# One load instead of four for the last V tile, and 256 rows of w4 in loads of 62, 2 and 64 partitions

## The chip, the cores and the metric

The kernel runs on one core of a Trainium2 chip. The metric is the device time of one execution in microseconds (us). Before the change the median of three runs is 196.03 us (195.90 to 196.08).

## The reference

One token is decoded for a batch of 8, with a width of 512. The first half is attention over a window: 32 query heads share 8 key/value heads, and of a cache of 8192 positions only the last 2048 count. The second half is a gated residual block whose token-shift branch is zero for a sequence of one token, so that w1 and w2 are never needed. What is left:

```
h  = x + attention(layernorm(x)) @ wo          # K and V: 8 x 8 x 2048 x 128 bf16 each
z  = layernorm(h)
x1 = z                                         # the shifted parts are zero for S = 1
h2 = h + x1 + gelu(layernorm(x1) @ w3) @ w4    # w3: 512 x 1792, w4: 1792 x 512
```

All arrays are bf16. The K and V windows are 67 MB of the 79 MB that the kernel reads.

## The kernel before

**Tiles.** K and V come in 16 units each (`NUN` = 16: 8 batches by 2 halves of the key/value heads). A unit is a load of 2 MB: 128 partitions, 16 KB in each, one contiguous run per partition. `knat` and `vnat` hold four such units each. Every unit of K is turned on the PE (line 305), moved out of PSUM by ACT and DVE (lines 292 and 293), and multiplied with the queries (line 320). After the softmax of a batch, V is multiplied with the probabilities (`pe_PV`, line 411 for the last three units, line 421 for the others).

**Order of the work.** There is no planner. Each engine has a list of operations written out by hand, and `Engine.emit` puts a wait in front of an operation where its list of (semaphore, value) pairs asks for one. All large loads are issued from SP's queue in one order: wq, then K and V units in turn (V three units behind K), the first half of wo at units 5 and 9, and at the end V of units 13, 14 and 15, the second half of wo in four pieces, w3 in four pieces, w4 in four pieces. An SP load waits until the buffer that it writes is free; the w3 and w4 loads go into the K buffers 0 and 1, which are free long before.

**The last V unit.** `load_v` loads units 0 to 14 in one DMA with runs of 16 KB. Unit 15 is loaded in four DMAs (lines 478 to 480), each a quarter of the columns, with runs of 4 KB per partition and a semaphore each (`sem_vl`). `V(n, w)` (line 396) gives `pe_PV` the semaphore for quarter w, so the PE can start on a quarter when it has landed.

**w4.** w4 has 1792 rows, that is 14 blocks of 128. Rows 0 to 1535 come in three DMAs of 512 rows: partition p gets four consecutive rows, a run of 4 KB. The first two have one semaphore (`sem_w4a`, wait for 32), the third `sem_w4b`. The last 256 rows come in a fourth DMA, two rows, 2 KB, per partition (lines 610 and 611, `sem_w4c`). In what follows these are called w4a (two pieces), w4b and w4c.

**The end of the chain.** After V the PE adds wo (line 498), DVE and ACT make the two layer norms (lines 619 to 649), the PE multiplies with w3 (line 639), DVE and ACT make the gelu in two halves (lines 655 and 657), and the PE multiplies with w4 (line 667) in groups that wait in this order: 32 blocks of 128x128 for `sem_w4a` and the gelu, 16 for `sem_w4b`, 8 for `sem_w4c`. Then come an addition, a turn, a copy and the store of 8 KB.

Of the kernel before, what the change touches and what calls it, by code (L numbers as in the profile page):

```python
# [21 lines left out]
F = 1792  # L22
FC = F // 128
# [7 lines left out]
U = 4  # L31
RR = 32
NCU = W // RR
UL = NCU * DH

NK = 4
NV = 4
# [44 lines left out]
def bass_sequential_preLN__sliding_block_cached__mixer_s_mlp__decode_kernel(  # L82
# [19 lines left out]
    NUN = NB * NU  # L102
# [4 lines left out]
    with es:  # L107
        sb = lambda shape, dtype, name: es.enter_context(nc.sbuf_tensor(name, shape, dtype))
        ps_t = lambda shape, dtype, name: es.enter_context(nc.psum_tensor(name, shape, dtype))
        S = lambda name: es.enter_context(nc.semaphore(name))  # L110

        knat = sb([128, NK, UL], dt.bfloat16, "knat")
        vnat = sb([128, NV, UL], dt.bfloat16, "vnat")
# [4 lines left out]
        w4_sb = knat[:, 1, 0:FC * D].rearrange("p (c n) -> p c n", c=FC)  # L118
# [49 lines left out]
        def tl(n, bf=False):  # L168
# [19 lines left out]

        sem_k = [S(f"sem_k{i}") for i in range(NK)]
        sem_v = [S(f"sem_v{i}") for i in range(NV)]  # L190
        sem_vl = [S(f"sem_vl{i}") for i in range(U)]
        sem_wl = [S(f"sem_wl{i}") for i in range(2)]
        sem_x, sem_wq, sem_wo, sem_w3, sem_w4a, sem_w4b, sem_w4c, sem_out = (
            S(n) for n in ("sem_x", "sem_wq", "sem_wo", "sem_w3", "sem_w4a", "sem_w4b", "sem_w4c", "sem_out"))
        PE, AC, DV, PO, SP = (Engine(S(n)) for n in ("s_pe", "s_act", "s_dve", "s_pool", "s_sp"))

        def dma(eng, dst, src, sem, *waits):
            def f(e):
                e.dma_start(dst, src).then_inc(sem, 16)  # L199
            eng.op(f, *waits, inc=False)  # L200
# [81 lines left out]
        e_T, e_Tlo, e_Thi, e_lo, e_hi, e_QK, e_PV = {}, [], [], [], [], {}, {}  # L282
# [111 lines left out]
            e_rL[b] = DV.op(lambda e: e.tensor_tensor(rLk[:, s, :, :], r_bc, k_bc, ALU.mult), e_r, e_mK)  # L394

        def V(n, w):
            if n == NUN - 1:
                return sem_vl[w], 16
            return sem_v[n % NV], 16 * (n // NV + 1)

        e_ev_o, e_fold = {}, {}
# [1 line left out]
        def pe_PV(i):  # L403
            n, w = divmod(i, U)
            b, t = divmod(n, NU)

            def f_last(e):
                for c in range(16):
                    cc = 8 * (w % 2) + c // 2
                    o = 256 * (cc // 2) + 32 * (4 * t + 2 * (w // 2) + c % 2) + cc % 2  # L410
                    ins = e.matmul(oT_ps[:, 0:16], vnat[:, n % NV, (16 * w + c) * DH:(16 * w + c + 1) * DH],  # L411
                                   pS[:, b % 2, o:o + 31:2], start=(w == 0 and c == 0), stop=(w == U - 1 and c == 15),
                                   skip_group_check=True)
                return ins

            def f(e):
                for c in range(8):
                    cc = 8 * (w % 2) + c
                    o = 256 * (cc // 2) + 32 * (4 * t + 2 * (w // 2)) + cc % 2
                    q = c % TO  # L420
                    ins = e.matmul(oT_ps[MO * q:MO * (q + 1), NO * (n % 2):NO * (n % 2 + 1)], pS[:, b % 2, o:o + 2 * MO - 1:2],  # L421
                                   vnat[:, n % NV, (16 * w + 2 * c) * DH:(16 * w + 2 * c + 2) * DH],
                                   start=(w == 0 and c < TO), stop=(w == U - 1 and c >= 8 - TO),
                                   tile_position=(0, MO * q), skip_group_check=True)
                return ins
            e_PV[i] = PE.op(f if n < NUN - NST else f_last, V(n, w), *e_pS[b],
                            e_ev_o.get(n - 1), e_sc[n - 1] if n > NUN - NST else None)
# [44 lines left out]
        def load_v(n):  # L472
            b, t = divmod(n, NU)
            src = A_v_cache[b, J * t:J * (t + 1), W0:SK, :].rearrange("j (r c) d -> r j (c d)", r=RR)
            if n < NUN - 1:
                dma(SP, vnat[:, n % NV, :], src, sem_v[n % NV], e_PV.get(U * (n - NV + 1) - 1))
                return
            for w in range(U):
                cs = slice(w * UL // U, (w + 1) * UL // U)
                dma(SP, vnat[:, n % NV, cs], src[:, :, cs], sem_vl[w], e_PV.get(U * (n - NV + 1) - 1))  # L480

        def load_wo(m, sem, g=2):
            dma(SP, wo_v[:, m:m + g, :, :].rearrange("p g k n -> p g (k n)"),
# [51 lines left out]
        for n in range(NUN):  # L535
# [4 lines left out]
            if n >= LVD:  # L540
                load_v(n - LVD)
            if n in WO_AT:
                load_wo(WO_G[WO_AT.index(n)], sem_wo)
            i = U * n
# [35 lines left out]
        for n in range(NUN - LVD, NUN):  # L580
            load_v(n)
# [22 lines left out]
            dma(SP, w3_sb[:, k, :], B_w3[128 * k:128 * (k + 1), :], sem_w3, e_T[U * (NUN - NK + 1) - 1])  # L604
        FA = 12
        w4_a = B_w4[0:FA * 128, :].rearrange("(a p c) n -> p a (c n)", p=128, c=4)
        for a, sem in ((0, sem_w4a), (1, sem_w4a), (2, sem_w4b)):
            dma(SP, w4_sb[:, 4 * a:4 * a + 4, :].rearrange("p c n -> p (c n)"), w4_a[:, a, :], sem,
                e_T[U * (NUN - NK + 2) - 1])
        dma(SP, w4_sb[:, FA:FC, :].rearrange("p c n -> p (c n)"),  # L610
            B_w4[FA * 128:F, :].rearrange("(p c) n -> p (c n)", c=FC - FA), sem_w4c)

        v3 = lambda t: t.rearrange("p (n b) -> p n b", b=B)
        vr = lambda t: t.rearrange("p (n b) -> p b n", b=B)
# [38 lines left out]
        for n in range(2):  # L653
            cs = slice(n * FH * B, (n + 1) * FH * B)
# [5 lines left out]
        for lo, hi, waits in ((0, FH, (e_gT[0], e_exp[NB - 1], (sem_w4a, 32))),  # L660
                              (FH, 8, (e_gT[1],)),
                              (8, FA, ((sem_w4b, 16),)),
                              (FA, FC, ((sem_w4c, 16),))):
            def pe_w4(e, lo=lo, hi=hi):
                for fc in range(lo, hi):
                    for nb in range(KC):
                        ins = e.matmul(z_ps[:, nb * B:(nb + 1) * B], w4_sb[:, fc, nb * 128:(nb + 1) * 128],
                                       gT[:, fc * B:(fc + 1) * B], start=(fc == 0 and nb == 0),
                                       stop=(fc == FC - 1), skip_group_check=True)
                return ins  # L670
            e_z = PE.op(pe_w4, *waits)
# [44 lines left out]
```

## Time and profile before

| | |
|---|---|
| median of three runs | 196.03 us |
| the profiled execution's own time | 195.93 us |
| its span in the trace | 194.6 us |
| DMA: bytes, mean over the span | 79.46 MB, 408 GB/s |
| share of the span in which PE / DVE / ACT are busy | 75% / 51% / 46% |
| last landing of w3 | 187.44 us |
| last landing of w4a, w4b, w4c | 189.95, 191.22, 191.85 us |
| last PE block of w4 ends | 192.29 us |

Times of single events count from the start of the span. The trace holds, for every DMA, when it was issued and when each of its 16 increments of the semaphore landed; a load is there when the last of the 16 has landed. It also holds every packet that the DMA engines moved, with start, duration and bytes, but not the number of the engine. The packets of one engine follow each other closely: the next one starts 3 to 4 ns before the one before has ended. As every engine has its own offset, the 16 chains can be told apart, and are called chain 0 to 15 here, in the order in which they began with wq.

### The profile page before, as it was taken

The numbers are of one execution on the slowest core, as the hardware profiler recorded it, in microseconds if no ns is written. First come the engines' busy times: TensorE is split into PE (matmuls) and PEld (weight loads), VectorE is DVE, ScalarE is ACT, GpSimd is POOL, SyncE is SP. The second block draws the span as 40 slices with busy tenths as digits, with TensorE's granted clock in tenths as the row PEclk, the third lists the DMA queues.
The fourth block names the chain that finished last, engine by engine and source line by source line (L and its number), as shares of the span: only waits on it lengthen the run. The fifth ranks groups of instructions, "written<-read, shape, count | busy, mean of one in ns | idle before, by whom it ended". The sixth has DMA issues, their size and how long they took to land.

```text
span 194.6 us, 4466 instructions
## 1 busy us (share of the span) xinstructions
PE 145.5 (75%) x1971; PEld 114.9 (59%) x1971; DVE 99.8 (51%) x256; ACT 89.2 (46%) x113; POOL 7.4 (4%) x28
## 2 busy tenths in 40 slices
PE   0038985988999794969497988785597896878764
PEld 0037852665777564756495857473585674767753
DVE  5402444784767492649055385565255865631130
ACT  6000565863847453655244646472264564150040
POOL 5001001001000100010001000100000000000000
PEclk9999999999999999999669699999799999555555
DMA  6999999999999999999999999999999999999981
GB/s 217 431 431 431 428 431 431 424 431 426 424 404 448 428 426 424 431 418 424 428 414 428 424 428 424 431 421 426 428 428 428 431 424 428 415 401 406 407 352 51
DMA packets 7538, 79.46 MB, mean 408 GB/s; under 512 B 856, under 2 KB 864, under 8 KB 3424
## 3 DMA queue, kind: packets, MB, share of 16 engines
q1 hardware_dynamic: 7504, 79.18, 96.9%
q8 instruction: 15, 0.25, 0.5%
q14 instruction: 3, 0.02, 0.0%
q10 hardware_dynamic: 16, 0.01, 0.0%
HBM read 79.18 MB, written 0.01 MB: 407 GB/s over the span
## 4 chain that ended last, share of the span: by engine, by line
DMA 51%; PE 30%; DVE 9%; SPq 6%; ACT 2%; issue 2%
DMA knat<-in_A_k_cache_dram 43%; PE kT_ps L305 18%; DMA knat<-in_B_w_dram 8%; SPq L199 6%; PE S_ps L320 5%; DVE kT_sb L293 5%; PE kT_ps L377 3%; DVE mcol L330 1%; DVE Pz L366 1%; PE sm L439 1%; ACT kT_sb L292 1%; ACT P_sb L351 1%; DVE Mrow L336 1%; PE sm L334 1%; PE sm L385 1%
## 5 line engine op out<-in xcount | busy, mean ns | idle before, releaser
L292 ACT ACTIVATE kT_sb<-kT_ps 128x1024 bf16<-128x1024 bf16 x64 | 62.8, 1023 | 43.4 <-PE kT_ps L305 43.4
L305 PE MATMUL kT_ps<-perm_k,knat 128*128 128x128 f32 x512 | 71.6, 298 | 11.3 <-DMA knat<-in_A_k_cache_dram 10.8
L305 PEld LDWEIGHTS kT_ps<-perm_k,knat 128*128 128x128 f32 x512 | 63.6, 154 | 19.0 <-DMA knat<-in_A_k_cache_dram 13.0
L293 DVE TENSOR_SCALAR kT_sb<-kT_ps 128x512 int32<-128x512 int32 x64 | 43.7, 689 | 37.7 <-PE kT_ps L305 37.7
L320 PE MATMUL S_ps<-kT_sb,qz 128*32 128x512 bf16 x256 | 19.9, 384 | 6.7 <-DVE kT_sb L293 3.9
L366 DVE TENSOR_TENSOR Pz<-P_sb,mJ 128x256 bf16<-128x256 bf16 x64 | 23.9, 416 | 0.0
L421 PE MATMUL oT_ps<-vnat,pS 128*32 128x256 bf16 x416 | 17.7, 280 | 0.9 <-DMA vnat<-in_A_v_cache_dram 0.9
L430 ACT ACTIVATE oE<-oT_ps 128x256 f32<-128x256 f32 x13 | 5.0, 384 | 27.4 <-PE oT_ps L421 27.4
L292 ACT ACTIVATE pS<-kT_ps 128x1024 bf16<-128x1024 bf16 x8 | 8.2, 1024 | 10.3 <-PE kT_ps L377 10.3
L421 PEld LDWEIGHTS oT_ps<-vnat,pS 128*32 128x32 bf16 x416 | 9.3, 97 | 4.1 <-DMA vnat<-in_A_v_cache_dram 1.0
L320 PEld LDWEIGHTS S_ps<-kT_sb,qz 128*32 128x32 bf16 x256 | 4.6, 94 | 11.6 <-ACT kT_sb L292 10.9
L293 DVE TENSOR_SCALAR pS<-kT_ps 128x512 int32<-128x512 int32 x8 | 5.5, 692 | 10.2 <-PE kT_ps L377 10.2
L377 PE MATMUL kT_ps<-perm_p,Pz 128*128 128x128 f32 x64 | 9.6, 298 | 0.0
L377 PEld LDWEIGHTS kT_ps<-perm_p,Pz 128*128 128x128 f32 x64 | 7.6, 151 | 3.0 <-issue 3.0
L259 PE MATMUL S_ps<-xlnT,wbig 128*128 128x8 bf16 x128 | 3.6, 168 | 7.7 <-DMA wbig<-in_A_wq_dram 7.7
L277 POOL COPY qz<-q_sb 64x64 bf16<-64x64 bf16 x16 | 4.6, 290 | 117.5 <-PE S_ps L320 101.7
L330 DVE TENSOR_REDUCE mcol<-S_ps 128x1 f32<-128x512 f32 x8 | 5.5, 692 | 5.8 <-PE S_ps L320 5.8
L259 PEld LDWEIGHTS S_ps<-xlnT,wbig 128*128 128x128 bf16 x128 | 3.5, 104 | 7.7 <-issue 7.7
L439 PEld LDWEIGHTS sm<-selo,oE 128*128 128x128 f32 x52 | 7.6, 211 | 0.4 <-ACT oE L430 0.4
L439 PE MATMUL sm<-selo,oE 128*128 128x16 f32 x52 | 7.6, 260 | 0.3 <-DVE negcol L348 0.3
L411 PE MATMUL oT_ps<-pS,vnat 128*128 128x16 bf16 x192 | 6.2, 174 | 1.7 <-DVE oK L445 1.0
L411 PEld LDWEIGHTS oT_ps<-pS,vnat 128*128 128x128 bf16 x192 | 5.9, 105 | 2.4 <-DMA vnat<-in_A_v_cache_dram 1.2
(90 smaller groups left out, 84.7 us busy)
## 6 DMA issues: line engine op xcount, KB each, us to landing
knat<-in_A_k_cache_dram SPq DMA_DIRECT2D x16, 2048.0 KB, 30.2
vnat<-in_A_v_cache_dram SPq DMA_DIRECT2D x15, 2048.0 KB, 34.3
wbig<-in_A_wq_dram SPq DMA_DIRECT2D x1, 4096.0 KB, 12.2
wbig<-in_A_wo_dram SPq DMA_DIRECT2D x2, 1024.0 KB, 33.0
vnat<-in_A_v_cache_dram SPq DMA_DIRECT2D x4, 512.0 KB, 10.8
wbig<-in_A_wo_dram SPq DMA_DIRECT2D x4, 512.0 KB, 12.6
knat<-in_B_w_dram SPq DMA_DIRECT2D x4, 448.0 KB, 13.6
knat<-in_B_w_dram SPq DMA_DIRECT2D x3, 512.0 KB, 15.1
```

Source lines behind the costliest of these rows:

```text
L199: e.dma_start(dst, src).then_inc(sem, 16)
L259: ins = e.matmul(S_ps[0][:, h * B:(h + 1) * B], wq_v[:, kc, h * DH:(h + 1) * DH], xlnT[:, kc * B:(kc + 1) * B], start=(kc == 0), stop=(kc ...
L292: e_lo.append(AC.op(lambda e: e.activation(dst[:, 0:1024], ps[:, 0:1024], ACT.Copy), e_Tlo[k], *free))
L293: e_hi.append(DV.op(lambda e: e.tensor_single_scalar(dst[:, 1024:2048].bitcast(dt.int32), ps[:, 1024:2048].bitcast(dt.int32), 0, ALU.bitwi ...
L305: ins = e.matmul(ps[:, c * 128:(c + 1) * 128], src[:, c * 128:(c + 1) * 128], perm_k[:, :], is_transpose=True)
L320: ins = e.matmul(S_ps[b % 2][32 * j:32 * (j + 1), :].rearrange("p (c r) -> p c r", c=16), qz[:, b % 2, J * t + j, k, lo:lo + 32], kT[:, j, k],
L330: e_max[b] = DV.op(lambda e: e.tensor_reduce(mcol[:, :], S_ps[b % 2][:, :], AX.X, ALU.max), e_QK[4 * b + 3], e_mT.get(b - 1))
L366: e_Pz[b, part] = DV.op(lambda e, o=o, p_bc=p_bc, m_bc=m_bc: e.tensor_tensor(Pz[:, 0, J * o:J * (o + 64)].rearrange("p (x j k) -> p x j k" ...
L377: ins = e.matmul(ps[:, c * 128:(c + 1) * 128], src[:, c * 128:(c + 1) * 128], perm_p[:, :], is_transpose=True)
L411: ins = e.matmul(oT_ps[:, 0:16], vnat[:, n % NV, (16 * w + c) * DH:(16 * w + c + 1) * DH], pS[:, b % 2, o:o + 31:2], start=(w == 0 and c = ...
L421: ins = e.matmul(oT_ps[MO * q:MO * (q + 1), NO * (n % 2):NO * (n % 2 + 1)], pS[:, b % 2, o:o + 2 * MO - 1:2], vnat[:, n % NV, (16 * w + 2 ...
L439: ins = e.matmul(sm[:, 32:48], oE[:, o:o + 128], selo[:, 16 * s:16 * s + 16], start=(s == 0), stop=(s == 2 * VP - 1))
```

## The change

V of unit 15 is loaded as the other units are, in one DMA with runs of 16 KB, with the semaphore of its buffer; `sem_vl` is gone, and all of unit 15's products wait for the whole unit. w4c is cut into three DMAs by partitions: 0 to 61, 62 and 63, and 64 to 127. The first two are issued after w3 and ahead of w4a; the third is issued last, where w4c was. All three count on `sem_w4c`, and the last eight PE blocks wait for 48 instead of 16.

```diff
-        sem_vl = [S(f"sem_vl{i}") for i in range(U)]
...
         def V(n, w):
-            if n == NUN - 1:
-                return sem_vl[w], 16
             return sem_v[n % NV], 16 * (n // NV + 1)
...
         def load_v(n):
...
-            if n < NUN - 1:
-                dma(SP, vnat[:, n % NV, :], src, sem_v[n % NV], e_PV.get(U * (n - NV + 1) - 1))
-                return
-            for w in range(U):
-                cs = slice(w * UL // U, (w + 1) * UL // U)
-                dma(SP, vnat[:, n % NV, cs], src[:, :, cs], sem_vl[w], e_PV.get(U * (n - NV + 1) - 1))
+            dma(SP, vnat[:, n % NV, :], src, sem_v[n % NV], e_PV.get(U * (n - NV + 1) - 1))
...
         w4_a = B_w4[0:FA * 128, :].rearrange("(a p c) n -> p a (c n)", p=128, c=4)
+        w4_c = B_w4[FA * 128:F, :].rearrange("(p c) n -> p (c n)", c=FC - FA)
+        for a, z in ((0, 62), (62, 64)):
+            dma(SP, w4_sb[a:z, FA:FC, :].rearrange("p c n -> p (c n)"), w4_c[a:z, :], sem_w4c,
+                e_T[U * (NUN - NK + 2) - 1])
         for a, sem in ((0, sem_w4a), (1, sem_w4a), (2, sem_w4b)):
             dma(SP, w4_sb[:, 4 * a:4 * a + 4, :].rearrange("p c n -> p (c n)"), w4_a[:, a, :], sem,
                 e_T[U * (NUN - NK + 2) - 1])
-        dma(SP, w4_sb[:, FA:FC, :].rearrange("p c n -> p (c n)"),
-            B_w4[FA * 128:F, :].rearrange("(p c) n -> p (c n)", c=FC - FA), sem_w4c)
+        dma(SP, w4_sb[64:128, FA:FC, :].rearrange("p c n -> p (c n)"), w4_c[64:128, :], sem_w4c)
...
-                              (FA, FC, ((sem_w4c, 16),))):
+                              (FA, FC, ((sem_w4c, 48),))):
```

## The prediction

> **What bounds the kernel now.** I read the slices of the page first.
>
> ```profile
> DMA  6999999999999999999999999999999999999981
> GB/s 217 431 431 431 428 431 431 424 431 426 424 404 448 428 426 424 431 418 424 428 414 428 424 428 424 431 421 426 428 428 428 431 424 428 415 401 406 407 352 51
> DMA packets 7538, 79.46 MB, mean 408 GB/s; under 512 B 856, under 2 KB 864, under 8 KB 3424
> ```
>
> The DMA engines are busy in every slice until the last two, so the time is set by bytes, by what a packet costs, and by what follows the last landing. The chain that ended last says which landing:
>
> ```profile
> 176.01 15.22 DMA knat<-in_B_w_dram
> 191.22 0.05 issue
> 191.27 0.59 PE S_ps L667 x16
> 191.86 0.04 issue
> 191.90 0.39 PE S_ps L667 x8
> ```
>
> It is w4b, at 191.22. The sixteen blocks that wait for it end at 191.86; w4c landed at 191.85, so the last eight follow with no more gap than an issue. The DMA view of 187 to 192 us, in 40 slices, shows how the end is reached:
>
> ```profile
> DMA  9899999896765666647469344443334332100000
> ...
> q8 instruction: 1, 0.02, 1.3%
> ```
>
> From 188 on the share falls in steps: engines run dry one after the other. The 16 increments for w4c land at 188.39 to 188.73 (six of them), 189.46, 190.10, 190.38, 190.84, and 191.50 to 191.85 (six). The packet records say why. In the run there are 15 instruction fetches of 16 KB (q8) and 3 of 8 KB (q14); a fetch of 16 KB takes 1.0 to 1.1 us, holds up the engine's own packets and leaves it about 1.1 us behind for good. Followed along the chains, q8 goes round eight engines in a fixed order (chains 5, 10, 6, 14, 3, 13, 11, 8), q14 hits two more (9, 9 and 1), and six are never hit (0, 2, 4, 7, 12, 15). Those six finish 3.3 us early. The stage behind w4 is this, in the timeline:
>
> ```profile
> 187.22 1.28 ACT L657 ACT_TABLE_LOAD   x1
> ...
> 187.49 1.97 PE L639 MATMUL kT_ps<-Pz,knat 128*128 128x8 bf16 x56 [0.75 <-DMA knat<-in_B_w_dram]
> ...
> 188.87 0.25 ACT L657 ACTIVATE Pz<-Pz 128x56 bf16<-128x56 f32 x1 [0.36 <-DVE Pz L655]
> ...
> 190.09 0.99 PE L667 MATMUL S_ps<-Pz,knat 128*128 128x8 bf16 x32 [0.62 <-ACT Pz L657]
> ...
> 191.27 1.01 PE L667 MATMUL S_ps<-Pz,knat 128*128 128x8 bf16 x24 [0.18 <-DMA knat<-in_B_w_dram]
> ```
>
> The wait before 190.09 is put down to ACT, but the gelu had ended at 189.12; w4a landed at 189.95.
>
> **The change, part by part.** The sum is made against the profiled execution: 195.93 us, of which 1.3 lie outside the span of 194.6. The median, 196.03, is 0.10 higher.
>
> *V of unit 15 in one load.* In the packet records a 4 KB packet follows the last after 158.2 ns, a 16 KB one after 610, a semaphore's after 6. Each engine spent 32 x 158.2 + 4 x 6 = 5.09 us on this unit and will spend 8 x 610 + 6 = 4.89: everything behind it lands 0.20 us earlier. (The first landings of units 13, 14 and 15 bear it out: 164.35, 169.25, 174.34.) SP issues three DMAs fewer (0.60 us each), in a queue that is ahead of the data by 10 to 15 us: nothing.
>
> The four quarters landed by 174.03, 175.31, 176.59 and 177.87; the PE began on the first at 176.79 and was through at 178.88. Now it begins when the whole unit is there, 177.87 - 0.20 + 0.05 = 177.72, and needs the same 2.09: 179.81, or 0.93 later. Behind it on the PE stand wo (line 498), the layer norm's sums and w3. What covers this: the first w3 block waited 0.75 us for w3's landing at 187.44 while its input was ready at 185.53, so 0.93 later is still in time for 187.24. On ACT the gelu's table load moves from 187.22 to 188.15, the first gelu ends at 189.68 instead of 189.12, and w4a lands at 189.75: hidden, with 0.1 us to spare. If more is lost on the way, it is paid one for one (rival 3).
>
> *w4c by partitions.* A packet of 2 KB follows the last after 80.5 ns. The piece of 64 to 127 gives each of 16 engines 4 packets instead of 8, so a late engine ends 0.32 us earlier: w4c at 191.85 - 0.20 - 0.32 = 191.33. But w4b lands at 191.02, and its 16 blocks run to 191.66: w4c is no longer waited for, and is worth 0.04 us at most.
>
> *The 62 rows.* How many engines take them? The trace has one short load: x, 8 rows, had 8 data packets and 8 semaphore packets on 8 engines, one row each. In every load the engines have equal shares (each chain holds 466 packets). Equal shares of 62 rows are possible on 2 engines with 31 each or on one; the 2 rows then go to two as well. Bounds: spread over 16 engines, 4 rows are 0.32 us; on two, 32 rows. I take two, since no load here has unequal shares. [...]
>
> On those two, w4a and w4b now stand behind 32 x 80.5 + 12 = 2.59 us more. This is the lower bound. The upper one comes from whether another engine can write a partition at full speed while the engine that always serves it is writing. In all loads with 128 partitions each engine has its own eight, so the trace never shows two engines on the same ones. An engine runs at 16384 B / 610 ns = 26.9 GB/s; if that is also what its partitions can take, two share it and a row costs 161 ns, 32 rows 5.15 us. The nearest row is x: five 1 KB rows for neighbouring partitions set out their semaphore packets within 41 ns (one packet alone is 44 ns) but land over 90 ns, 2.08 to 2.17; the 16 increments of the output store are 13 ns apart. They seem to queue. I take the upper bound less the four rows for an engine's own partitions: 28 x 161 + 4 x 80.5 + 12 = 4.84 us. [...]
>
> The sum, if the two are never-hit engines: their w4a ended at 186.04 to 186.34 (second piece, before its 0.42 us to landing), so it lands at 186.04 - 0.20 + 4.84 + 0.42 = 191.10 to 191.40. The 32 blocks run from 191.15 to 192.14. w4b, 1.27 later, lands at 192.37 to 192.67; its blocks run from 192.42 to 193.01. The last piece, 4 rows more, lands 0.33 to 0.65 later at 192.7 to 193.3, the eight blocks end at 193.44 to 193.7 instead of 192.29: **+1.15 to +1.45, I take +1.3**: 197.2, 197.3 against the median.
>
> SP issues two DMAs more (0.43 to 1.09 us each by the rows at 168 to 179 us) but is 10 us ahead; without that lead they would cost up to 2.2 us. The longer wait (48) stands last on the PE, nothing is queued behind it but the tail, which is unchanged.
>
> **The rivals.**
>
> 1. *The two engines are never-hit ones and write at full speed.* Then w4b is at 187.74 - 0.20 + 2.59 = 190.1 on them, ahead of the late engines' 191.02, and the end is 191.02 + 0.05 + 0.59 + 0.39 = 192.05: -0.24 us, 195.8 (-0.12%). For it: 3.3 us of idle time fit 2.59. It decides as long as a row costs under 115 ns (3.68 us from 187.54 to 191.22, by 32). Spreading 62 rows over many engines gives the same 195.8.
> 2. *One of the two is an engine that fetches.* Six chains of 16 end 3 us later than the idle ones. At 80.5 ns a row, w4b lands at 191.02 + 2.59 = 193.61, the end is 194.68: +2.4, 198.4; with sharing up to 200.7. Chain 1 or 9 (q14) lies between: 196.0 to 198.9. [...] I give it 0.22.
> 3. *Unit 15's later start is not hidden.* There is an idle stretch of 1.05 us in wo at 179.56 with nothing waited for, after a fetch (178.12 to 179.20). If the delay of 0.93 brings on another such gap, the gelu is 1.0 late beyond its cover and the w4 blocks run without waits from 190.8 to 192.8: +0.5, 196.5.
>
> **How the numbers follow.** A change of 0.2% (0.39 us) is about what can be told from none. Forecast (two prompt engines, shared writing) 0.40; rival 1 with the spread rows 0.33; rival 2 0.22; rival 3 0.05. Rival 1 gains less than 0.2%, so most of it is "same", some 0.07 of it faster if more than 0.39 is gained. Slower: 0.40 + 0.22 + 0.04 = 0.66. The likeliest one's own range is 196.6 (sharing costs 70%) to 197.8. To hold 8 in 10 the range goes from 195.7 (rival 1) to 198.8 (rival 2 without sharing); the rest of rival 2 is left out above, a larger gain below.
>
> **What would show it.** In the changed profile: the packets under 8 KB fall from 3424 by some 550 (unit 15's 512 data packets and 48 of semaphores go); first landing of unit 15 at 174.14; the 62-row load has 62 packets with two late increments; where the two chains spend 160 ns per 2 KB packet, the forecast holds, at 80 rival 1. PE's L667 groups then wait for w4a and w4b at 191 and 192. If the last engines of w4b are chains with two fetches and 32 rows, it was rival 2. Wrong altogether: w4b landing earlier than 191.02 on all engines, or a PE that waits for wo, not for w4.

## The result and the profile after

The changed kernel takes 197.14 us (median of six runs, 197.05 to 197.59) against 196.03 before: a ratio of 1.0061, 95% interval 1.0051 to 1.0072. The profiled execution took 197.29 us, its span is 196.0, 1.4 more than before.

The page of the changed kernel (DMA rows, all 40 slices):

```profile
DMA  6999999999999999999999999999999999999980
GB/s 236 428 421 428 435 428 428 428 428 426 421 415 428 428 428 423 428 425 428 420 426 428 428 428 428 428 421 426 425 425 428 431 425 428 425 413 395 378 265 35
DMA packets 7110, 79.46 MB, mean 405 GB/s; under 512 B 812, under 2 KB 820, under 8 KB 2868
```

Up to the 37th slice it is nearly the same kernel. In the 38th and 39th (4.9 us each) the engines are as busy as before, and move 378 and 265 GB/s where they had moved 407 and 352. The packets under 8 KB are 556 fewer: the single load of V has 560 fewer, and the new loads of w4 have 4 more of semaphores.

The chain that ended last, in order of time:

```profile
178.18 14.64 DMA knat<-in_B_w_dram
192.82 0.05 issue
192.86 0.82 PE S_ps L662 x24
```

It still ends in w4b, which landed at 192.82 instead of 191.22. w4c's last piece landed at 192.97, in time for the last eight blocks, so the PE's last 24 blocks follow without a gap. The timeline of the tail (start, duration, operation, idle time before it and what ended that):

```profile
177.85 0.60 PE L408 MATMUL oT_ps<-pS,vnat 128*128 128x16 bf16 x16 [1.27 <-DMA vnat<-in_A_v_cache_dram]
...
178.51 1.45 PE L408 MATMUL oT_ps<-pS,vnat 128*128 128x16 bf16 x48
...
188.28 1.99 PE L634 MATMUL kT_ps<-Pz,knat 128*128 128x8 bf16 x56 [1.38 <-DMA knat<-in_B_w_dram]
...
191.32 1.00 PE L662 MATMUL S_ps<-Pz,knat 128*128 128x8 bf16 x32 [1.05 <-DMA knat<-in_B_w_dram]
...
192.86 0.81 PE L662 MATMUL S_ps<-Pz,knat 128*128 128x8 bf16 x24 [0.55 <-DMA knat<-in_B_w_dram]
```

The PE now starts V of unit 15 at 177.85, as the sum had it (177.72). Then it waits for data three times: for w3 until 188.28 (before: 187.49), for w4a until 191.32 (190.09), for w4b until 192.86 (191.27). That w3 is late is the sign to follow up: the w3 loads stand ahead of the new loads in the queue. It does not set the end itself: both halves of the gelu had ended by 190.81, and w4a landed at 191.18.

The start of wo, before:

```profile
179.00 0.56 PE L498 MATMUL S_ps<-o,wbig 128*128 128x8 bf16 x15
180.62 1.47 PE L498 MATMUL S_ps<-o,wbig 128*128 128x8 bf16 x49 [1.05 <-issue]
```

and after:

```profile
180.09 2.15 PE L490 MATMUL S_ps<-o,wbig 128*128 128x8 bf16 x64
```

One stretch, 185 to 188.5 us, with the busy time (and number of instructions) of PE, its weight loads, DVE, ACT and POOL, the granted clock, and two columns on DMA; before the change:

```profile
185.00:188.50 3.50, 1.91 (x34) 1.73 (x34) 1.43 (x8) 1.70 (x3) 0.00 (x0) 0.50 0.97 384
```

and after it:

```profile
185.00:188.50 3.50, 1.27 (x10) 1.09 (x11) 1.43 (x8) 1.54 (x3) 0.00 (x0) 0.50 1.02 290
```

The last two columns are the share of time in which the DMA engines are busy and the GB/s. All 16 are busy and move a quarter less. In the packet records the chains of two engines each show 31 packets of 2 KB, a semaphore's, one more of 2 KB: one chain from 183.56 to 186.90, the other from 184.24 to 187.76. From 185.5 until about 189 most packets take 1.2 to 1.7 times their usual time (0.16 us for 4 KB before the change), and they do so on all 16 chains alike (up to 188, 1.4 to 1.6 times in the mean of each chain).

### The profile page after: what moved, and what is told of

It reads as the page before. It is cut to its first block, busy times and chain, and to the rows that moved or that the text cites. A ratio compares the mean times of both kernels' runs of the same rounds, so it can differ in the third digit from the quotient of the medians.

```text
span 196.0 us, 4465 instructions
## 1 busy us (share of the span) xinstructions
PE 146.9 (75%) x1971; PEld 116.4 (59%) x1971; DVE 99.5 (51%) x256; ACT 89.6 (46%) x113; POOL 7.4 (4%) x28
## 4 chain that ended last, share of the span: by engine, by line
DMA 52%; PE 28%; DVE 9%; SPq 7%; ACT 2%; issue 2%
DMA knat<-in_A_k_cache_dram 44%; PE kT_ps L304 16%; DMA knat<-in_B_w_dram 7%; SPq L198 7%; PE S_ps L319 5%; DVE kT_sb L292 5%; PE kT_ps L376 3%; DVE mcol L329 1%; DVE Pz L365 1%; ACT kT_sb L291 1%; PE sm L436 1%; ACT P_sb L350 1%; DVE Mrow L335 1%; PE sm L333 1%; PE sm L384 1%
## 5 line engine op out<-in xcount | busy, mean ns | idle before, releaser
L304 PE MATMUL kT_ps<-perm_k,knat 128*128 128x128 f32 x512 | 72.9, 302 | 10.8 <-DMA knat<-in_A_k_cache_dram 10.4
L304 PEld LDWEIGHTS kT_ps<-perm_k,knat 128*128 128x128 f32 x512 | 65.1, 157 | 18.2 <-DMA knat<-in_A_k_cache_dram 12.5
```

The costliest lines, as they stand in the source:

```text
L304: ins = e.matmul(ps[:, c * 128:(c + 1) * 128], src[:, c * 128:(c + 1) * 128], perm_k[:, :], is_transpose=True)
```

## The experiments

Theory 1: rows for partitions that another engine serves are what slows. Theory 2: two engines with long queues of short rows slow the rest, whichever the partitions. Besides, V's later start could be the cost.

**The two parts alone.** The V part alone is the change without its w4 edits; the w4 part alone is the change with `sem_vl` and the four V loads put back.

> V of unit 15 in one load, w4 as before. By my theory (the loss is all in the w4 loads) everything behind unit 15 lands 0.20 us earlier, the PE starts unit 15 at 177.8 instead of 176.8 and is covered, and the time falls by 0.2 us to about 195.8. By the rival that the later start of unit 15 costs the time: 0.5 to 1.0 us slower than before, w3 or the gelu waiting for the layer norm.

> w4's last rows as in the changed kernel (62, 2, 64), V of unit 15 in four loads as before. By my theory the whole loss is here: 197.2 to 197.4, 0.2 above the changed kernel at most, and the data moved per us falls to some 260 to 350 GB/s for 3 to 4 us from the moment the two loads begin. By the rival that V costs the time: 195.9 to 196.1.

V alone: 195.80 us (median of 11) against 196.06, ratio 0.9993 (0.9984 to 1.0002). w4 alone: 197.47 us, ratio 1.0074 (1.0059 to 1.0090). The loss is in the w4 loads: +1.41 there and -0.26 for V make +1.15, and the change measured +1.11. The -0.26 is a difference of medians; the interval of V alone includes 1, so that a gain is not shown, but a loss of 0.5 us or more is excluded. In the profile of V alone, unit 15 starts on the PE at 177.85 and the PE later waits 1.14 us for w3 (before: 0.75); its last landings are 187.72 for w3 and 191.48 for w4b in that execution, which was the second longest of its runs (196.14).

**Where the rows go.** All further kernels but the last are V alone with something added ahead of w4a. The first adds two loads of 2 partitions by 16 rows of 2 KB into spare buffers (the store at the end waits for them too; they have landed by then in every run):

```diff
+        for h in range(2):
+            dma(SP, knat[h:h + 5:4, 2:4, :].rearrange("p k (i n) -> p (k i) n", n=1024),
+                A_wo.rearrange("(g i t r) n -> g i t (r n)", i=16, t=2, r=2)[2 * h:2 * h + 2, :, 0, :], sem_d, e_T[NBLK - 1])
```

The second adds the same rows in the shape of the change, to 62 and 2 partitions:

```diff
+        for a, z in ((0, 62), (62, 64)):
+            dma(SP, knat[a:z, 2, 0:1024], A_wo.rearrange("(x t r) n -> x t (r n)", t=2, r=2)[a:z, 0, :], sem_d, e_T[NBLK - 1])
```

> V of unit 15 in one load and w4c in one load of 128 partitions (so e1), and ahead of w4a two extra loads of 2 partitions by 16 rows of 2 KB, into spare buffers, whose results nobody uses: again 32 rows on each of two engines, but into partitions 0, 1 and 4, 5, which by the even split of a 128-partition load may be the two engines' own. Theory 1 (foreign partitions are what slows): rows go at 80 ns each, no other engine slows, the two end about 2.6 us later, still before or with the late ones; 195.8 to 196.3. Theory 2 (two engines with long queues of 2 KB rows slow the rest, whatever the partitions): the same fall to 260 to 350 GB/s as in the changed kernel, 197.0 to 197.8.

> As the run with rows into partitions 0, 1, 4, 5, with the same source rows, but the extra loads go to partitions 0 to 61 and 62 to 63, one row of 2 KB each. Theory 1 and theory 2 both expect the fall in GB/s and 197.0 to 197.8; a third, that the w4 rows themselves or their place in memory are the cause, expects 195.8 to 196.3 here.

Into partitions 0, 1, 4, 5: 195.80 us, ratio 0.9989 (0.9980 to 0.9998), no loss at all. Into 0 to 63: 196.92 us, ratio 1.0046 (1.0032 to 1.0060). The 128 KB are the same, the source is the same, and so, by their place in time, are the two engines (each time one chain of 32 rows begins at 183.3 to 183.4, and a second about 0.75 later). With partitions 0, 1, 4, 5, 16 rows take 1.32 to 1.33 us on either, 83 ns each. The stretch of 185 to 188.5 again, with partitions 0, 1, 4, 5:

```profile
185.00:188.50 3.50, 2.23 (x38) 2.04 (x39) 1.44 (x9) 1.52 (x3) 0.00 (x0) 0.50 0.97 383
```

and with 0 to 63:

```profile
185.00:188.50 3.50, 1.11 (x15) 0.92 (x16) 1.43 (x8) 1.71 (x3) 0.00 (x0) 0.50 1.03 303
```

Theory 2 falls, and the loss comes without w4's own rows, their place in memory or their semaphore. What is left between the two is the partitions: either that most belong to other engines, or that every row has a new one.

**Foreign or many.** The same two loads again, into partitions 8, 9, 12 and 13, and later into 32, 33, 36 and 37:

```diff
-            dma(SP, knat[h:h + 5:4, 2:4, :].rearrange("p k (i n) -> p (k i) n", n=1024),
+            dma(SP, knat[8 + h:13 + h:4, 2:4, :].rearrange("p k (i n) -> p (k i) n", n=1024),
```

> As the run with rows into partitions 0, 1, 4, 5 (which measured 195.80 and no fall in GB/s), but into partitions 8, 9, 12, 13: still two engines, two partitions at a time and 16 rows of 2 KB in each, only that the partitions are ones that two other engines should serve. Theory 1 (foreign partitions): a fall in GB/s, rows of 100 to 160 ns, and 196.4 to 197.2. A theory that it is the many partitions (a new one with every row) expects no fall and 195.7 to 196.1.

> As the runs with rows into partitions 0, 1, 4, 5 (no fall) and 8, 9, 12, 13 (fall to 205 GB/s), now into 32, 33, 36, 37. If an engine's own partitions are eight in a row (0 to 7, 8 to 15), these are foreign: a fall to about 205 GB/s and some 198.2. [...]

Partitions 8, 9, 12, 13: 198.21 us, ratio 1.0103 (1.0086 to 1.0120), the slowest of all and 1 us beyond the range that theory 1 was given. Partitions 32, 33, 36, 37: 195.80 us, ratio 0.9985 (0.9974 to 0.9996). In the stretch of 185 to 188.5, with 8, 9, 12, 13:

```profile
185.00:188.50 3.50, 1.19 (x4) 1.00 (x4) 1.69 (x10) 1.19 (x3) 0.00 (x0) 0.50 1.01 200
```

and with 32, 33, 36, 37:

```profile
185.00:188.50 3.50, 1.88 (x35) 1.69 (x35) 1.42 (x8) 1.71 (x3) 0.00 (x0) 0.50 0.96 380
```

So it is not the number of partitions, which is four each time: it is which four (198.21 us with 8, 9, 12, 13, and 195.80 with each of the other two sets). Nothing else about 8, 9, 12 and 13 is slow, as every load of 128 partitions writes them too, and there no chain falls behind other than by a fetch. The reading that fits these runs is that the two engines' own partitions include 0, 1, 4, 5 and 32, 33, 36, 37, and not 8, 9, 12, 13, so that they are not eight in a row. It is an inference: the trace has no numbers of engines or partitions that would show it packet by packet. While the two engines wrote into 8, 9, 12 and 13, their rows took 160 to 190 ns, twice 80.5 as the upper bound had it, and the core moved 200 GB/s, about half of the 376 of V alone, with all 16 engines busy (share 1.01).

**One engine.** One added load of 31 partitions by one row, which equal shares put on a single engine (it has one late increment):

```diff
+        for a, z in ((0, 31),):
+            dma(SP, knat[a:z, 2, 0:1024], A_wo.rearrange("(x t r) n -> x t (r n)", t=2, r=2)[a:z, 0, :], sem_d, e_T[NBLK - 1])
```

> V of unit 15 in one load and w4c in one load of 128 partitions, and ahead of w4a one extra load of 31 partitions by one row of 2 KB, which equal shares put on one engine alone. If every foreign row takes its loss from all engines, half of the loss of the run with 62 and 2 rows is left: a fall in GB/s to some 330 to 370 and 196.2 to 196.5. If the loss needs two such writers at a time, no fall below 390 and 195.7 to 196.0.

196.15 us, ratio 1.0004 (0.9995 to 1.0014). That is 0.35 us more than V alone by the medians, just under the range; the intervals of the two overlap, so the time alone does not prove a loss. The stretch shows it (V alone: 376 GB/s):

```profile
185.00:188.50 3.50, 1.06 (x14) 0.89 (x14) 1.43 (x8) 1.71 (x3) 0.00 (x0) 0.50 1.02 354
```

Cut finer, the packet records have 322 to 330 GB/s from 185 to 187 while the load passes, and 401 right after it (before the change: 400 to 412 throughout). It did not take two such writers: while one engine's 31 rows passed, the whole core slowed to those 322 to 330 GB/s.

**Two loads of 64 partitions.** Not two engines, but 16 with four rows each, with w4's own rows:

```diff
+        dma(SP, w4_sb[0:64, FA:FC, :].rearrange("p c n -> p (c n)"), w4_c[0:64, :], sem_w4c,
+            e_T[U * (NUN - NK + 2) - 1])
...
+        dma(SP, w4_sb[64:128, FA:FC, :].rearrange("p c n -> p (c n)"), w4_c[64:128, :], sem_w4c)
```

> V of unit 15 in one load; w4's last rows in two loads of 64 partitions, the first ahead of w4a, the second last, so that each has 16 engines with 4 rows each, and half or more of the rows still go to partitions that another engine serves. If the loss comes from rows of foreign partitions as such (128 rows, twice as many as in the changed kernel's first two loads are foreign here at most), the GB/s fall while they pass and the time is 196.3 to 197.5. If it needs two engines that do nothing else for 3 us, each engine's 4 rows cost 0.3 to 0.65 us once, the engines are at different places, and the time is 195.7 to 196.2.

197.37 us, ratio 1.0067 (1.0052 to 1.0082): no better than the change, though no engine has more than its even share. In the packet records the GB/s dip to 311 at 184, 282 at 185.5 and 243 at 187.5, as the engines come to their four rows one group after another. Here the form of the load cost 1.25 us (197.37 against 196.12 before), and no pair of engines carried it.

This bears on the changed kernel too, whose third piece, partitions 64 to 127, is such a load. On five of the six early engines its rows pass from 187.75, as the last of the 64 rows ahead of w4a ends, to 188.7, and packets stay slow: from 188.5 to 189 they take 1.4 times their usual time in the median. With the same 64 rows but w4c in one load (the run with partitions 0 to 63) they are back at 1.0 by then. In the three kernels with a load of 64 to 127, w4b also lands 0.61 to 0.83 us after its last packet, in the seven others after 0.43 to 0.45. What this piece is worth in time was not tried by itself: 1.0061 for the change and 1.0046 without it have intervals that overlap.

No version here is clearly better than the kernel before. V alone and the two kernels with rows in partitions 0, 1, 4, 5 and 32, 33, 36, 37, which hold the same V edit, all have a median of 195.80, 0.13 to 0.15% below, and the intervals of two of the three end just below 1.

## Why the prediction came true, and where its steps did not

The forecast was 197.3 us, +1.3; it measured 197.14, and in the profiled execution +1.36. The last w4 block was to end at 193.44 to 193.7, and ended at 193.68. The parts, in their order:

- **V in one load: right.** Unit 15's first landing was to be 174.14 and is 174.09. The PE's delay was to be 0.93 and hidden. It was: alone, the edit gave -0.26 (the sum had -0.24), within the noise. But it was not hidden where the sum had it. Ahead of w3 on the PE's list stands the layer norm's second sum (line 643), which ended at 186.75 before; 0.93 later is 187.68, not in time for 187.24. What took up the delay was wo: in the changed kernel it runs from 180.09 to 182.24 with no gap like the 1.05 us of before, and the layer norm begins at 184.62 instead of 184.46. So rival 3 fell, and the cover was hardly needed.
- **How many engines: right.** The estimate from equal shares held. In the changed kernel two chains have 31 rows and one row each, and `sem_w4c` shows two late increments for each of the two loads (187.61, 187.85, 188.55 and 188.78); the trace has the others in two records, at 173.43 and 177.22, before any of these rows moved (183.56). The load of 31 rows shows one late increment, the pair of loads with 32 rows each on two engines shows two each.
- **Which engines: nearly.** Both were forecast as engines that are never hit by a fetch. One is; the other began the new rows 0.68 us later, as the chain does that the 8 KB fetch at 74.1 us had held up once. That is the case of chain 1, the milder one of rival 2 (196.0 to 198.9 for chains 1 and 9); its main case, a chain that fetches by q8, did not occur. The chance of 0.22 was the author's estimate: no trace from before the change shows which engines a load of 62 rows takes.
- **What a row costs: the mis-sized term.** "28 x 161 + 4 x 80.5 + 12 = 4.84 us" on each of the two. No run shows the four rows that this sets apart for an engine's own partitions. Measured: 31 rows in 3.20 and 3.41 us, 103 and 110 ns a row, so about 3.5 us in all. That is neither of the two signs, 160 or 80, and under the 115 ns up to which rival 1 (195.8) was to decide. A row did take twice as long at two fixed partitions of 8, 9, 12 and 13 (160 to 190 ns), but rows that moved on to a new partition each time got by with these 103 to 110; why is not shown.
- **Who pays: the step that failed.** The sum left the other engines alone, with w4b landing at 191.02 on the late ones, and had the two engines set the end with 192.37 to 192.67. In fact all 16 engines slowed (packets took 1.4 to 1.6 times as long in the mean of each chain, 185.5 to 188). w3, forecast for 187.24, landed at 188.24. Followed along the chains, the last w4b packet of the latest other engine ends at 191.87, against 190.79 before, and that of the slower of the two at 191.99: both set the end, 0.12 us apart. Then w4b landed at 192.82, 0.83 us after its last packet; before it was 0.43, and the sum had 0.42.
- **w4c's relief: right and worthless.** The last blocks still follow w4b without a gap. That packets stay slow while the third piece passes (1.4 times from 188.5 to 189) was not in the sum.

So the side and the size were right, and that the partitions decide was shown (195.80 against 198.21 us); two engines at the same partitions is the reading that fits, not one that a trace shows. The account of who loses was wrong. That the totals agree is luck in part. The rows took 1.3 us less than the sum had, one of the two engines came 0.68 later, the other engines lost 1.1 where the sum had them gain 0.20, and the landing came 0.4 later.

## What to carry to other kernels

Do not count the idle time of a few DMA engines as a reserve that any load can use: here what counted was which partitions a row was for (the same 128 KB took 195.80 us into 0, 1, 4, 5 and 198.21 into 8, 9, 12, 13). In this kernel w4c in one load of 128 partitions did better (V alone, ratio 0.9993) than cut into 62, 2 and 64 (1.0061) or 64 and 64 (1.0067), while cutting unit 15 by columns cost 0.26 us by the medians, with an interval that includes none. So, of a stream of 128 partitions, try cuts by columns before cuts by partitions, where other loads are running. And read a stretch near the end by GB/s beside the busy share: here, 290 GB/s instead of 384 at a share of 1.02 was the sign of the loss, which no list of waits names.

## What the runs showed of the hardware that was not expected

- More than the two engines with the new rows lost time. From 185 to 188.5 the changed kernel moved (384 - 290) x 3.5 = 329 KB less than before, for 64 rows of 2048 B, 131 KB. With two engines' rows in partitions 8, 9, 12 and 13 the core ran at 200 GB/s, with the rows in 32, 33, 36 and 37 at 380, both times with all 16 engines busy (shares of 1.01 and 0.96). Why all 16 chains slow alike was not tried, and stays open.
- As many rows cost nothing in partitions 0, 1, 4, 5 or 32, 33, 36, 37: 128 KB more, and 195.80 us both times, as for V alone.
- An instruction fetch of 16 KB left one DMA engine about 1.5 us behind, not the 1.1 us that it took itself: behind the fetch of 178.21 to 179.30 in the changed kernel, that engine's next two packets of 4 KB took 0.43 and 0.36 us instead of 0.16. The fetches went round eight engines. Six had two of them by the end of w4 and six had none: before the change, w4c's increments land from 188.39 to 191.85, 3.5 us between the first engine and the last.
- Where rows for partitions 64 to 127 came as a load of their own, right behind w4b, w4b landed 0.61 to 0.83 us after its last packet instead of 0.43 to 0.45.
